# Two upright score tiles of a fused attention and feed-forward kernel made ordinary, and the order around them written anew

## The chip, the cores and the metric

The kernel runs on one core of a Trainium2 chip. A core has five engines with queues of their own: PE (matrix products), DVE and POOL (elementwise work and reductions), ACT (exponentials, casts) and SP, which here issues all DMAs. Each engine takes its instructions strictly in the order of its queue. The metric is the device time of one execution in microseconds; beside it stands one profiled execution.

## The reference, cut to what matters

```python
mask = q_assign[:, :, :, None] == k_assign[:, :, None, :]
scores = scale * np.matmul(q, k.transpose(0, 1, 3, 2))
scores = np.where(mask, scores, -1000000000.0)
scores = scores - np.max(scores, axis=-1, keepdims=True)
attn = np.exp(scores)
attn = attn / (np.sum(attn, axis=-1, keepdims=True) + 1e-09)
return np.matmul(attn, v).astype(np.float32)
...
h = x @ w_in
g = np.maximum(h, 0.0) + np.log1p(np.exp(-np.abs(h)))
return (g @ w_out).astype(np.float32)
```

q, k and v are 4 x 8 x 768 x 64 in float32, the two weight matrices come in float64; `q_assign` and `k_assign` are the nearest of 16 centroids per head. The attention's output, 3072 x 512, goes through a layer of 2048 hidden columns with softplus.

## The kernel before, in words

The work is cut into eight passes: a batch and one half of its 768 queries (three blocks of 128). A pass has 24 score tiles, one per head and query block, numbered through the program; tiles 24 to 47 are the second pass. Floats are split into a high and a low float16 part, so that a product is made of two or three float16 products. Besides the scores a pass makes, from the attention of its 24 tiles, 16 blocks of hidden rows (`ffn1`, f = 0 to 15, two halves each), their softplus, and the output (`ffn2`). The weights are converted and split step by step (`prep_weights`, steps 0 to 31) beside the first two passes. While tiles 34 to 47 are made, the hidden rows of the first pass and the weight steps 24 to 31 are worked on.

A score tile is made in one of two ways.
- Ordinary (`scores`): four products of 128x384 (L1051, scores of t), the row maximum on DVE (L1067), the exponential on ACT (L1075), its high part by a cast (L276, key `ph{t}`), the low part by a subtraction (L1089, key `p{t}`) on POOL or DVE, then one transposing DMA for a pair of tiles (L1101), and the attend: 18 float16 products (L1141 to L1143).
- Upright (`upright`): two products of 128x384 for the maxima (L942), the maximum on DVE (L954), a transposition of it on PE (L961), a shift row written by ACT or DVE (L967, L969, key `u{t}`), twelve products of 128x128 that give the scores already transposed (L981, L982), the exponential on ACT (L1025), and the attend in float32 (L1137). It needs no cast, no subtraction and no DMA.

Pairs of tiles listed in `UPRIGHT` are upright (`is_up`): pair 17 is tiles 34 and 35, head 3 with query blocks 4 and 5. An ordinary tile among upright neighbours needs a row of its query tile filled with zeros (`fill`, L798).

Scores are written to a ring of two PSUM buffers (tag `s`), hidden rows and cluster products to another ring of two (tag `h`), outputs to one buffer (tag `o`): a new product waits until the buffer's last reader is done. The hidden rows of f are read by an exponential and a logarithm on ACT (L1233, L1234) and a combination on DVE (L1249, here: the softplus of f), whose end frees the buffer.

The order of all operations is written out: `Order.run` walks the string `PLAN`, two characters per operation, each naming the coroutine whose next operation is issued. Nothing is reordered later. `either` chooses the engine of an operation: the first of two named, or the second where its key stands in `SWAPPED`.

Of the kernel before, what the change touches and what calls it, by code (L numbers as in the profile page):

```python
# [38 lines left out]
REBASE = 2.0**-112
SIGN_UP = 2.0**32  # L40
# [8 lines left out]
    "2927270d2b22220a222925cdce25242b2b29272d29260d0dcccbcccecd2d2729292fcf222b28cc0ace2f2h2f0d2d2f2d2bcb22cccgch"
    "ci2h2j2a0d0d0dcgcg2b2h2dcf0dcf0d0dcd2j2c2d2f2e0dcf0dcf0d0d22cjcd2fcbcb2h2e2e2e2l2j2j0d0d2l2n2nchci2echcgch2g"  # L50
    "2h2h2j2l2n2lcgcgck2jch2nce2p2p2i2l2k2p2l2r2ncicicjci2p2rcdchcl2ncjcj2m2p2t2r0eckckckck2t2p2rcj2e2ecicmcjce2o"
    "2r2r2v2v2t2q2t2v2t2q2q2qcl2x0e0e0e2v2tck2q2q2s2v2v2x2z2z2x2xcmclcmclcm2ucn2q2z312x312w0e0e0e0e0e0e0eco2z2x2z"
    "cl2z330e333131cl2y310fcncn0ecncz33353531cmcmcpcq33czcncococo33dpcn35cz37370f0f0fcoczdqdqdp35303937320e0e0eco"
    "cr0e333537dpcz0hdqdqdq3232323439czcp32cqcpcpcqcq32323539370f0f3b3936dsdsdsczcpcp3739crcq3b0fcrcrcrcr393d0fcz"
    "3bcz3b0ecs3d3d3b0f0f0f3dczdtdt0h3bdudu0f0fdtdt0hcqdt383d0i3d3f3f3aczctcscsducs3f3h3f3f3c3jcz3edv3h3jcscs0gcu"
    "0i0i0i3h3ld03hdwctct3h3hdw3edwcz3j0g3n3e3e3edwczd0ctcu3l3ndv0i3j3l3pdydyct3e3edwd0cu0g0j0kcucu3l3n3ndyczczdz"
    "3gdz0i3p0i0icz3rczcuctcv3l3j3l3p3t3p0g3ndzczdz0i3r3iczdzd03p3pcve0e03t3r3v0ie0cz3ke10jcvcv3tcz3xcve13te23md0"
# [1634 lines left out]
```

## Time and profile before

| what | us |
|---|---|
| median of three runs | 813.47 (812.93 to 814.27) |
| the profiled execution | 813.45 |
| its span, first to last instruction | 811.7 |
| PE busy / DVE / ACT / POOL | 799.6 / 599.2 / 548.7 / 471.5 |

The span is what the trace shows; 1.75 us of the execution lie around it. Busy is time in which an engine has any instruction recorded. Records of PE overlap, so that its work is read from the distances between starts.

### The profile page before, as it was taken

Reading aid. Unit: us, or ns where it says so; the run is one execution under the profiler, and the core shown is the slowest. Engines: PE = TensorE matmul, PEld = TensorE weight load, DVE = VectorE, ACT = ScalarE, POOL = GpSimd, SP = SyncE. Lnnn points to the kernel's source line nnn. Section 1 sums busy time; section 2 is a strip of 40 time slices with the busy share of each in tenths; the row PEclk is TensorE's granted clock in tenths of the full one; section 3 lists DMA queues with packets and bytes.
Section 4 is the critical chain, followed back from the end, with each engine's and each line's share of the span. In section 5 each row is a group of like instructions: output and inputs, shape, how many; then the busy total and the mean of one; then the engine's idle time right before and its main releaser. Section 6 shows DMA issues by size and latency. Waiting matters only on the chain.

```text
span 811.7 us, 19601 instructions
## 1 busy us (share of the span) xinstructions
PE 799.6 (99%) x8086; PEld 542.6 (67%) x8086; DVE 599.2 (74%) x1005; ACT 548.7 (68%) x851; POOL 471.5 (58%) x351
## 2 busy tenths in 40 slices
PE   8999999999999999999999999999999999999998
PEld 7898976655666666666666656666666656576787
DVE  6889998987976877756675547658555878887795
ACT  6677688865777777648587577677676667645441
POOL 4645455554756577745677685687578552613454
PEclk9999999999999999999999999999999999999999
DMA  9986769999899999999899999999888677830101
GB/s 259 234 184 165 205 151 216 195 227 204 165 190 182 180 202 196 215 204 177 153 177 177 185 185 175 209 203 179 171 159 176 116 143 131 131 60 1 47 1 59
DMA packets 390474, 133.71 MB, mean 165 GB/s; under 512 B 367088, under 2 KB 383984, under 8 KB 390384
## 3 DMA queue, kind: packets, MB, share of 16 engines
q1 hardware_dynamic: 390384, 132.46, 82.6%
q8 instruction: 63, 1.03, 0.5%
q14 instruction: 27, 0.22, 0.1%
HBM read 35.68 MB, written 6.29 MB: 52 GB/s over the span
## 4 chain that ended last, share of the span: by engine, by line
PE 76%; DMA 4%; DVE 3%; ACT 2%; issue 1%; POOL 0%; SPq 0%; DVEq 0%; POOLq 0%; ACTq 0%
PE s L1051 11%; PE h L1212 9%; PE h L1214 9%; PE h L1213 9%; PE o L1613 7%; PE o L1615 7%; PE o L1614 7%; DMA pt<-phl 4%; PE mbank L1141 3%; PE mbank L1143 3%; PE mbank L1142 3%; PE m L1490 2%; PE m L1492 2%; PE m L1491 2%; ACT phl L276 1%
## 5 line engine op out<-in xcount | busy, mean ns | idle before, releaser
L1089 POOL TENSOR_TENSOR phl<-p,phl 128x768 f16<-128x768 f32 x117 | 194.1, 1667 | 124.1 <-ACT phl L276 94.1
L1067 DVE TENSOR_REDUCE negm<-s 128x1 f32<-128x768 f32 x156 | 148.1, 953 | 50.3 <-PE s L1051 48.8
L1075 ACT ACTIVATE p<-s,negm 128x768 f32<-128x768 f32 x156 | 139.4, 896 | 64.4 <-DVE negm L1067 49.1
L1212 PE MATMUL h<-xT,wi 128*128 128x384 f16 x512 | 166.9, 326 | 1.1 <-DVE fg L1249 1.1
L1214 PE MATMUL h<-xT,wi 128*128 128x384 f16 x512 | 167.1, 326 | 0.0
L1213 PE MATMUL h<-xT,wi 128*128 128x384 f16 x512 | 167.0, 326 | 0.0
L276 ACT CAST phl<-p 128x768 f16<-128x768 f32 x145 | 118.7, 828 | 20.3 <-DMA pt<-phl 18.0
L1051 PE MATMUL s<-kt,qt 128*128 128x384 f16 x624 | 126.2, 326 | 0.3 <-ACT p L1075 0.3
L1233 ACT ACTIVATE fa<-h 128x384 f32<-128x384 f32 x128 | 62.2, 487 | 70.9 <-PE h L1214 70.2
L1613 PE MATMUL o<-wo,gh 128*128 128x512 f16 x288 | 109.2, 379 | 0.4 <-DVE ot L1636 0.4
L1615 PE MATMUL o<-wo,gh 128*128 128x512 f16 x288 | 109.2, 379 | 0.0
L1614 PE MATMUL o<-wo,gh 128*128 128x512 f16 x288 | 109.2, 379 | 0.0
L1249 DVE SCALAR_TENSOR_TENSOR fg<-fa,h 128x384 f32<-128x384 f32 x104 | 56.7, 549 | 61.6 <-ACT fa L1234 54.2
L1141 PE MATMUL mbank<-vb,pt 128*128 128x65 f16 x936 | 100.2, 193 | 0.6 <-DMA pt<-phl 0.4
L1142 PE MATMUL mbank<-vb,pt 128*128 128x64 f16 x936 | 100.3, 192 | 0.0
L1143 PE MATMUL mbank<-vb,pt 128*128 128x65 f16 x936 | 100.0, 194 | 0.0
L1141 PEld LDWEIGHTS <-pt 128*128 128x128 f16 x936 | 86.8, 98 | 12.9 <-DMA pt<-phl 2.3
L1142 PEld LDWEIGHTS <-pt 128*128 128x128 f16 x936 | 86.3, 97 | 10.4
L1272 POOL TENSOR_TENSOR gh<-fg,gh 128x768 f16<-128x768 f32 x43 | 71.9, 1673 | 28.1 <-ACT gh L276 28.0
L1143 PEld LDWEIGHTS <-pt 128*128 128x128 f16 x936 | 86.4, 97 | 0.0
L1051 PEld LDWEIGHTS <-qt 128*128 128x128 f16 x624 | 58.4, 98 | 40.3 <-issue 0.6
L1214 PEld LDWEIGHTS <-wi 128*128 128x128 f16 x512 | 50.0, 98 | 33.2
(300 smaller groups left out, 1621.2 us busy)
## 6 DMA issues: line engine op xcount, KB each, us to landing
...
pt<-phl SPq DMA_TRANSPOSE x78, 6.0
```

What stands on the lines that cost most here:

```text
L1051: nc.tensor.matmul(st[:, j, :SH], qt[:, s, i], kt[:, s, NT // 2 * j : NT // 2 * (j + 1)], start=(s == 0), stop=(s == 1),)
L1067: yield op("DVE", 950, lambda: nc.vector.tensor_reduce(negm, st[:, :, :SH], AX.XY, ALU.max, negate=True))
L1089: lambda e: e.tensor_tensor(phl[:, u, 1], p32, phl[:, u, 0], ALU.subtract),
L1141: nc.tensor.matmul(av, pt[:, 0, c], vb[:, c, D : 2 * D + 1], start=(c == 0), stop=False)
L1142: nc.tensor.matmul(av[:, :D], pt[:, 0, c], vb[:, c, :D], start=False, stop=False)
L1143: nc.tensor.matmul(av, pt[:, 1, c], vb[:, c, D : 2 * D + 1], start=False, stop=(c == NT - 1))
L1212: nc.tensor.matmul(hp, w[0], x[0], start=(c == 0), stop=False)
L1213: nc.tensor.matmul(hp, w[0], x[1], start=False, stop=False)
L1214: nc.tensor.matmul(hp, w[1], x[0], start=False, stop=(c == NP - 1))
L1613: nc.tensor.matmul(po, g[0], wo[:, f, 0, 0], start=(f == f0), stop=False)
L1614: nc.tensor.matmul(po, g[0], wo[:, f, 0, 1], start=False, stop=False)
L1615: nc.tensor.matmul(po, g[1], wo[:, f, 0, 0], start=False, stop=(f == f0 + NF // 2 - 1))
```

## The change

Pair 17 leaves `UPRIGHT`, so tiles 34 and 35 become ordinary. The keys `u34` and `u35` are gone with it, `ph34`, `ph35`, `p34` and `p35` come (POOL makes both subtractions, ACT both casts), one transposing DMA and one zero fill come. In `SWAPPED`, `p40` goes (its subtraction moves from DVE to POOL) and `w24`, `w25` (weight subtractions, POOL to DVE), `wh27` (a weight cast, ACT to POOL) and `xh1_1` (a cast of 128x384, ACT to POOL) come. `PLAN` differs from about the 370th of 3464 operations to the 1418th, which before ran from some 66 us to some 295 us. No function is changed.

```diff
-UPRIGHT = (0, 1, 2, 3, 4, 5, 6, 7, 8, 9, 10, 11, 12, 13, 14, 15, 16, 17)
+UPRIGHT = tuple(range(17))
...
-    "d0cz0mebebeb0m0ld0d0ebebea0gec3w0g0g0gcycy0gcycy0g0g0gd03yd040ea0gcy0g0g0g0ld0420od0424242424242eded0n0n0n0n"
+    "czebebebd0d0d0ebebea0gec3w3y0g0g0gcycy0gcycy0g0g0gd0d0d0eacy0g0g0g0g0m0m0l0ld0ed40424242424242420o0n0n0n0n0n"
```

The attends of tiles 34 and 35 go further back on PE. Before, from the scores of tile 37 to those of tile 39 (`s_4`, `s_5` and `s_3` are tiles 37, 38 and 39; `ptf_4` holds tiles 34 and 35; one row of each group of products is shown):

```order
L1051 MATMUL s_4_2145<-kt_593,qt_1_1557 128x384
...
L1137 MATMUL mbank<-rawv_131,ptf_4_2064 128x65 x6
...
L1051 MATMUL s_5_2151<-kt_593,qt_1_1557 128x384
...
L1212 MATMUL h_5_2088<-xT_985,wi 128x384
...
L1137 MATMUL mbank<-rawv_131,ptf_4_2064 128x65 x6
...
L701 MATMUL cnt_2142<-eq_k_2020,ones 128x192
...
L1051 MATMUL s_3_2197<-kt_593,qt_1_1557 128x384
```

Now:

```order
L1051 MATMUL s_4_2103<-kt_593,qt_1_1558 128x384
...
L1051 MATMUL s_5_2131<-kt_593,qt_1_1558 128x384
...
L1212 MATMUL h_5_2078<-xT_985,wi 128x384
...
L701 MATMUL cnt_2122<-eq_k_2005,ones 128x192
...
L1051 MATMUL s_3_2164<-kt_593,qt_1_1558 128x384
```

Both rows of L1137 have left this stretch; they come back as float16 attends behind the second half of f = 6.

POOL around the same place, before (`phl` are low parts of scores, `wo` weights, `gh` hidden rows, `kn` keys, `xn` the attention's output):

```order
L404 TENSOR_TENSOR wo<-wo 128x512
L1272 TENSOR_TENSOR gh_1_2089<-fg_1_1990,gh_1_2089 128x768
L1089 TENSOR_TENSOR phl_3_2146<-p_4_3_2125,phl_3_2146 128x768
L404 TENSOR_TENSOR wo<-wo 128x512
L631 TENSOR_TENSOR kn_10_2116<-rawk_2113,kn_10_2116 128x12x64
L1089 TENSOR_TENSOR phl_3_2146<-p_4_4_2183,phl_3_2146 128x768
L1178 TENSOR_TENSOR xn_1_2239<-x_3_1_2237,xn_1_2239 128x2x3x64
L1272 TENSOR_TENSOR gh_2_2220<-fg_2_2084,gh_2_2220 128x768
L404 TENSOR_TENSOR wo<-wo 128x512 x2
```

Now:

```order
L276 CAST wo<-wo 128x512
L1089 TENSOR_TENSOR phl_4_2008<-p_3_4_2003,phl_4_2008 128x768
L1089 TENSOR_TENSOR phl_4_2008<-p_3_5_2042,phl_4_2008 128x768
L1089 TENSOR_TENSOR phl_3_2126<-p_4_3_2106,phl_3_2126 128x768
L631 TENSOR_TENSOR kn_10_2093<-rawk_2014,kn_10_2093 128x12x64
L1089 TENSOR_TENSOR phl_3_2126<-p_4_4_2151,phl_3_2126 128x768
L1272 TENSOR_TENSOR gh_1_2079<-fg_1_1994,gh_1_2079 128x768
L1272 TENSOR_TENSOR gh_2_2187<-fg_2_2097,gh_2_2187 128x768
L276 CAST wo<-wo 128x512
L404 TENSOR_TENSOR wo<-wo 128x512
L276 CAST xn_1_2320<-x_3_1_2311 128x2x3x64
L404 TENSOR_TENSOR wo<-wo 128x512
```

Three subtractions of scores stand in a row where a weight, a hidden row, a score and a weight stood; a cast of weights and one of `xn` are new.

DVE from the maximum of tile 35 to that of tile 36, before (`eq_k` and `best_k` are the cluster operations of keys, `fg` the softplus, `vb` the values):

```order
L954 TENSOR_REDUCE negu_5_2028<-m_5_2018 128x1
L590 TENSOR_TENSOR eq_k_2020<-eq_k_2020,tab 128x192
L592 TENSOR_REDUCE best_k_2066<-eq_k_2020 128x12
L594 TENSOR_TENSOR eq_k_2020<-eq_k_2020,best_k_2066 128x192
L969 TENSOR_SCALAR qt_1_1106<-turned 1x128
L650 TENSOR_SCALAR kn_8_1783<-eq_k_2020 128x12x16
L1249 SCALAR_TENSOR_TENSOR fg_1_1990<-fa_3_2036,h_3_1992 128x384
L467 TENSOR_TENSOR vb_104<-rawv_1879,vb_104 128x12x64
L404 TENSOR_TENSOR wo<-wo 128x512
L1067 TENSOR_REDUCE negm_3_2123<-s_3_2047 128x1
```

Now:

```order
L1067 TENSOR_REDUCE negm_5_2015<-s_5_2000 128x1
L404 TENSOR_TENSOR wo<-wo 128x512
L590 TENSOR_TENSOR eq_k_2005<-eq_k_2005,tab 128x192
L592 TENSOR_REDUCE best_k_2045<-eq_k_2005 128x12
L404 TENSOR_TENSOR wo<-wo 128x512
L594 TENSOR_TENSOR eq_k_2005<-eq_k_2005,best_k_2045 128x192
L650 TENSOR_SCALAR kn_8_1784<-eq_k_2005 128x12x16
L1249 SCALAR_TENSOR_TENSOR fg_1_1994<-fa_3_2032,h_3_1996 128x384
L467 TENSOR_TENSOR vb_104<-rawv_1880,vb_104 128x12x64
L1067 TENSOR_REDUCE negm_3_2104<-s_3_2076 128x1
```

The weight subtraction (L404) of step 24 now stands ahead of the cluster operations, that of step 23 between them instead of behind `vb`, and a shift row is gone.

ACT early in the second pass, before (`turned` is the transposed maximum; L967 writes shift rows; the three in a row are those of tiles 16, 18 and 17):

```order
L967 ACTIVATE qt_0_609<-turned 1x128 x3
L390 ACTIVATE wi<-wo 128x512
L1025 ACTIVATE ptf_1_1310<-u_1_1265 128x768
L1025 ACTIVATE ptf_1_1310<-u_2_1336 128x768
L832 ACTIVATE n_112<-eq_q_1_1331 128x12x16
L276 CAST wi<-wo 128x512 x2
L1025 ACTIVATE ptf_0_1379<-u_0_1366 128x768
L276 CAST wi<-wo 128x512
L967 ACTIVATE qt_0_609<-turned 1x128 x2
```

Now:

```order
L967 ACTIVATE qt_0_609<-turned 1x128 x2
L390 ACTIVATE wi<-wo 128x512
L1025 ACTIVATE ptf_1_1309<-u_1_1265 128x768
L1025 ACTIVATE ptf_1_1309<-u_2_1334 128x768
L832 ACTIVATE n_112<-eq_q_1_1329 128x12x16
L276 CAST wi<-wo 128x512 x2
L967 ACTIVATE qt_0_609<-turned 1x128
L276 CAST wi<-wo 128x512
L1025 ACTIVATE ptf_0_1403<-u_0_1390 128x768
L276 CAST wi<-wo 128x512
L967 ACTIVATE qt_0_609<-turned 1x128 x2
```

The shift row of tile 18 has moved behind the exponential of tile 17, the cluster row `n` and two weight casts. On PE the attend of tile 17 stands ahead of tile 18's products in turn.

## Rows read from the trace of the kernel before

**Rows 1.** the page, busy time and share of the span, x instructions
```profile
PE 799.6 (99%) x8086; PEld 542.6 (67%) x8086; DVE 599.2 (74%) x1005; ACT 548.7 (68%) x851; POOL 471.5 (58%) x351
```

**Rows 2.** PE in order of time, 153 to 156: start, length, line, operands
```profile
153.46 0.81 PE L1051 MATMUL s<-kt,qt 128*128 128x384 f16 x4
154.10 0.19 PE L1141 MATMUL mbank<-vb,pt 128*128 128x65 f16 x1
...
154.65 0.38 PE L1613 MATMUL o<-wo,gh 128*128 128x512 f16 x1
```

**Rows 3.** PE's waits, whole program: total us, times, longest
```profile
PE h L1212 <- DVE fg L1249: 1.1, 3, 0.6
...
PE turned L961 <- ACT qt L967: 0.7, 2, 0.4
PE turned L961 <- DVE rs L1158: 0.5, 1, 0.5
...
PE o L1613 <- DVE ot L1636: 0.4, 1, 0.4
...
PE s L1051 <- ACT p L1075: 0.3, 1, 0.3
```

**Rows 4.** busy us of PE, PEld, DVE, ACT, POOL; clock, DMA
```profile
112.00:158.00 46.00, 44.81 (x399) 30.75 (x398) 41.56 (x62) 38.21 (x62) 23.26 (x19) 1.00 0.91 204
```

**Rows 5.** the chain that ends at 157, from 112, by line
```profile
by line: DMA rawk<-in_k_dram 10.6%; DVE wo L392 10.2%; issue 9.7%; ACT phl L276 7.3%; DVE negm L1067 7.0%; DVE wo L396 6.0%; DVE phl L1089 5.6%; DVE fg L1249 5.6%; ACT p L1075 5.4%; DVE eq_k L590 3.3%; PE h L1212 2.5%; PE h L1213 2.2%; PE h
```

**Rows 6.** PE in order of time, 90 to 94
```profile
90.81 1.45 PE L1137 MATMUL mbank<-rawv,ptf 128*128 128x65 f32 x12
92.09 0.22 PE L981 MATMUL u<-qt,kt 128*128 128x128 f16 x1
...
92.77 0.49 PE L942 MATMUL m<-kt,qt 128*128 128x384 f16 x2
...
93.20 1.45 PE L1137 MATMUL mbank<-rawv,ptf 128*128 128x65 f32 x12
```

**Rows 7.** ACT in order of time, 125 to 130; [idle before <- ended by]
```profile
125.64 0.90 ACT L1075 ACTIVATE p<-s,negm 128x768 f32<-128x768 f32 x1 [0.28 <-DVE negm L1067]
...
128.45 0.83 ACT L276 CAST kn<-rawk 128x768 f16<-128x768 f32 x1 [0.49 <-DMA rawk<-in_k_dram]
129.19 0.89 ACT L1075 ACTIVATE p<-s,negm 128x768 f32<-128x768 f32 x1
```

**Rows 8.** groups by line: count, busy us, mean ns, idle before
```profile
L1089 POOL TENSOR_TENSOR phl<-p,phl 128x768 f16<-128x768 f32 x117 | 194.1, 1667 | 124.1 <-ACT phl L276 94.1 <-issue 14.1 <-PE sim_k L563 5.2
...
L1025 ACT ACTIVATE ptf<-u 128x768 f32<-128x768 f32 x36 | 29.2, 810 | 17.2 <-PE u L982 17.0
```

**Rows 9.** DVE in order of time, 119 to 134
```profile
119.31 1.01 DVE L590 TENSOR_TENSOR eq_k<-eq_k,tab 128x192 f16<-128x192 f16 x1
...
123.06 0.69 DVE L404 TENSOR_TENSOR wo<-wo 128x512 f16<-128x512 f32 x1
...
125.53 0.42 DVE L392 TENSOR_SCALAR wo<-wo 128x512 int32<-128x512 int32 x1
...
131.93 1.80 DVE L392 TENSOR_SCALAR wo<-wo 128x512 int32<-128x512 int32 x1 [1.47 <-ACT wo L390]
```

**Rows 10.** POOL in order of time, 119 to 134
```profile
119.05 1.16 POOL L404 TENSOR_TENSOR wo<-wo 128x512 f16<-128x512 f32 x1
...
131.81 1.64 POOL L1089 TENSOR_TENSOR phl<-p,phl 128x768 f16<-128x768 f32 x1
```

**Rows 11.** DMA issues by line: count, us from issue to landing
```profile
pt<-phl SPq DMA_TRANSPOSE x78, 6.0
```

**Rows 12.** PE in order of time, 126 to 132
```profile
126.71 0.81 PE L1051 MATMUL s<-kt,qt 128*128 128x384 f16 x4
...
128.64 0.81 PE L1051 MATMUL s<-kt,qt 128*128 128x384 f16 x4
...
131.64 0.81 PE L1051 MATMUL s<-kt,qt 128*128 128x384 f16 x4
```

More of the change, by code (lines that the diff above doesn't have):

```diff
@@ new lines @@
+SWAPPED = ('E1_0', 'S1l_1', 'S1l_3', 'S2_1', 'S2_3', 'S2h_0', 'S2l_0', 'S3l_0', 'S3l_2', 'S4_0', 'S4_2', 'S4_3', 'S4h_2', 'S4l_1', 'S4l_2', 'T1a_0', 'T1a_2', 'T1c_0', 'T1c_3', 'T1h_3', 'T1l_1', 'T2a_2', 'T2c_1', 'T3a_0', 'T3a_1', 'T3a_2', 'T3a_3', 'T3b_0', 'T3b_1', 'T3b_2', 'T3c_1', 'T3l_1', 'T3l_3', 'T4c_0', 'T4h_2', 'T4h_3', 'T4l_0', 'T4l_2', 'g0_3', 'g0_5', 'g1_1', 'g2_5', 'g5_7', 'g6_0', 'g6_1', 'g6_4', 'g6_5', 'g6_6', 'g7_1', 'g7_2', 'g7_4', 'g7_5', 'g7_6', 'g7_7', 'gh1_6', 'gh2_4', 'gh3_1', 'gh5_6', 'gh7_0', 'gh7_2', 'gh7_3', 'gh7_5', 'k0_0', 'k0_1', 'k14', 'k18', 'k22', 'kT0_0_0', 'kT0_2_1', 'kT1_2_0', 'kT1_2_1', 'm12_2_0', 'm12_3_0', 'm20_4_0', 'm28_7_0', 'm8_2_0', 'm8_3_0', 'p100', 'p101', 'p103', 'p136', 'p170', 'p172', 'p173', 'p175', 'p177', 'p178', 'p180', 'p181', 'p182', 'p183', 'p184', 'p185', 'p186', 'p189', 'p190', 'p191', 'p38', 'p39', 'p42', 'p45', 'p46', 'p47', 'p59', 'p61', 'p64', 'p67', 'p71', 'p72', 'p79', 'p82', 'p85', 'p89', 'p90', 'p92', 'ph175', 'ph178', 'ph180', 'ph184', 'ph186', 'ph189', 'ph58', 'ph62', 'ph83', 'ph86', 'ph87', 'q0_0_0', 'qT1_1', 'u1', 'u11', 'u13', 'u21', 'u23', 'u27', 'u31', 'u33', 'u35', 'v8', 'vh14', 'vh18', 'w15', 'w19', 'w20', 'w23', 'w24', 'w25', 'w29', 'wh17', 'wh24', 'wh27', 'wh29', 'wh30', 'wh7', 'wh9', 'x0_2', 'x2_0', 'x6_3', 'x7_0', 'x7_1', 'x7_2', 'x7_3', 'xh0_3', 'xh1_1', 'xh1_3', 'xh2_3', 'xh3_0', 'xh3_3', 'xh6_3', 'xh7_0', 'zk10', 'zk12', 'zk16', 'zk18', 'zk2', 'zk20', 'zk4', 'zq0_1', 'zq8_2')
@@ L48 @@
     "1xc7c6c61zc61xc8c7c7c6c721211w23231z0a21211z1y210d252023ce0bcfc9cac8cbcc21caca25252723c822c9c9c8ca2723c92325"
[L49 to L57, printed above, removed]
@@ L58 @@
-    "0j3vcvcw3t3re13x3r3t3v3z3zcze1e1e3e3e3e30k0k0k3x3ocze4cw3q3qcz413q3qcwcw0i3ze4e4e4cxcze53qd00n3x0i0i3ve5cwcz"
-    "cwe4d0cze7e73x3s3v3x3qe5e6d0410mcye7czczcxcxcxcxcxe60g3u0ke7e7e8d0e9e941410ke9cz0k0k0k0k0k413z3z410k0n0n3q0n"
-    "d0cz0mebebeb0m0ld0d0ebebea0gec3w0g0g0gcycy0gcycy0g0g0gd03yd040ea0gcy0g0g0g0ld0420od0424242424242eded0n0n0n0n"
-    "0n0n0n0n0l0l0n0kd0d04343434343eed045cz4545454545eeczef4747474747cz494949494949efd0egczeheh4b4b4b0o0oefd04d4d"
-    "4dehehd00l0l0l0l4f4f0l0ld04b4b4d4d4f444h4h4h4hd0eiei4j4j4j464dcz0l0l0l0l4h4l4l4f4fehczejejej48cz4a4hcz0l4n4n"
@@ L63 @@
-    "czcz4l4p0p0l4cekekek4p4ecz4e4l4l4j4j4lel4nekekelel4e4e4p4p4pczd0cz4g0p0pem4eemem4e4eem4n4nemczenen4r4r4r4ieg"
-    "4p4t4t4tczd0enen4v4v4r4r4k4x4x4t4t4v4v4v4x4mczeoeo4t4z4zczeoeo51514zczepep4o0p534q4qep4x4x4xcz51d04q4q4q4q53"
-    "535555eo4z4z4sczeq51510p574u514q57eqeq55czd0ereqeq0p0p0p0p57cz53534w59594yeseses5555550p0p5b5b0p0p0p0p0p0pd0"
+    "2927270d2b22220a222925cdce25242b2b29272d29260d0dcccbcccecd2d2729292fcf222b28cc0ace2f2h2f0d2d2d2bcb22cccgch2h"
+    "2j2a0d0d0dcgcg2b2h2dcf0dcf0d0dcd2j2c2d2e2e2ecg2e0dcf0dcicf0d0d0d22cjce2f2fcd2fcbcb2h2l2j2j0d0d2l2n2nchcichch"
@@ new lines @@
+    "2h2g2h2j2l2n2lcgcgck2jch2n2p2p2e2e2i2l2k2p2l2r2ncicicjci2p2rchcl2ncjcj2m2p2t2r0eckckckckcd2t2p2rcj2ecicmcjce"
+    "2o2r2r2v2v2t2q2t2v2t2q2q2qcl2x0e0e0e2t2vck2q2q2s2v2v2x2z2z2x2xcmclcmclcm2ucn2q2z312x312w0e0e0e0e0e0e0eco2z2x"
+    "2zcl2z330e333131cl2y310fcncn0ecncz33353531cmcmcpcq33czcncococo33dpcn35cz37370f0f0fcoczdqdqdp35303937320ecocr"
+    "33350e0e0e0e37dpcz0hdqdqdq3939323232czcp32cqcpcpcqcq32323534370f390f3b36dsdsdscpcp37cr3b0f3bcq3d0fcrcrcrczcz"
+    "cz3b3dcr0f0fcz39cq0fdtdt0h3ddu0f39dt3b3d0h3d380icsdu0f3f3f3aczctcsducscs3f3h3f3d3f3jczdv3hcscs3j0gcu0i0i0i3h"
@@ new lines @@
+    "3ld0ctdx3hct3h3hdxdtdxcz3jdx0g3nczdydyctcudt3c3ed03l3n0gdvdycz0i3l3j3pctdxd03ecu0j3e0kcucucu3l3e3n3ncvczdz3r"
+    "0i0idz0i3e3p3jcz3g3iczct3l3l3p3t3p0g0idzczdz3r3nczdzd03p3pe0e03t3r3vcve0czcz3ke10i0jcvcv3t3t3xcve1e23md00j3e"
+    "3vcvcw3t3re13x3r3t3v3z3zcze1e1e3e3e3e30k3z0k0k3xcz3ocwe43q3qcz413q0i3qcwcwe4e4e4e4cxcze5e5e53qd0d00n3x0i0i3v"
+    "cwczcwcze7e73x3s3v3x3qe6d0410mcye7czczcxcxcxcxcxe60g3u0ke7e7e8d0e9e941410ke9cz0k0k0k0k0k413z3z410k0n0n0n3e3q"
+    "czebebebd0d0d0ebebea0gec3w3y0g0g0gcycy0gcycy0g0g0gd0d0d0eacy0g0g0g0g0m0m0l0ld0ed40424242424242420o0n0n0n0n0n"
@@ new lines @@
+    "0n0n0n0n0kd0d0d0ee43430l0l43434345d0cz4545454545eeczeg474747474749czed4949eg494949efczeheh4b4b4b0o0oegd04d4d"
+    "4dehehd00l0l0l0l4f4f0l0ld04b4b4d4d4f444h4h4h4hd04j4j4j464dcz0l0l0l0l4h4l4l4f4fehczejeieiejej48cz4a4hcz0l4n4n"
+    "4l4p0p0l4cekczczekek4p4ecz4e4l4l4e4e4j4j4l4nelekekelel4p4p4pczd0cz4g0p0pem4eemem4e4eem4n4nemczenen4r4r4r4i4p"
+    "ef4t4t4tczd0enen4v4v4r4r4k4x4x4t4t4v4v4v4x4mczeoeo4t4z4zczeoeo51514x4zczepepep4o0p534q4q4x4xcz51d04q4q4q4q53"
+    "535555eo4z4z4sczeq51510p574u514q57eqeq55czd0ereqeq0p0p0p0p57cz53534w59594yeses5555es550p0p5b0p5b0p0p0p0p0pd0"
@@ L68 @@
     "0q0q0q0q0qd05t5g5n5r5td05i5p5p5pexex0q0qex5r5v5vez5t5t5t0q5v5r5r5k5x5xcz5m5tczf0f0f00r0r5xex5z5z5z5v5vczd0cz"
-    "f1f1f15x5x5o61cz6161635q5q5q5q5q5q610r63czf2f2f2d05x65655scz5z5z0r610r0r0r0r0t0u6367czd05u6165f3f1f169f3670r"
+    "f1f1f15x5x5ocz5q5q61635q61615q5q5q610r63czf2f2f2d05x65655scz5z5z0r610r0r0r0r0t0u6367czd05u6165f3f1f169f3670r"
     "f30r695wcz63635yczd0f36565650t0t670u0u0s0uf4f4f469cz6b6b6bczf6f66d0w6df667676d5qcz60czf7f76b6d62626262f569f3"
```

1 line of the change is left out of this document (removed).

## The prediction

> **What bounds the kernel now.** I read the engines' shares first: PE has a record running for 799.6 of 811.7 us, at the full granted clock (the 2.4 GHz level), the next engine DVE for 599.2 [rows 1]. That share cannot be read as work, because records overlap: the records of four score products span 0.81 us, yet the next group begins 0.64 us after they did [rows 2]. So I read starts, not durations, and then PE's waits: those that fall in or near this change's stretch (66 to 295 us) are 1.1 for DVE's softplus, 0.7 for ACT's shift rows, 0.5 for DVE's row sums and 0.4 for DVE's accumulator, all small [rows 3]. By that, PE is the bound and whatever leaves PE leaves the time. The stretch in which tiles 34 to 46 are made says something else. From 112 to 158 us DVE is busy 41.6 of 46 and ACT 38.2 [rows 4], and the chain that ends there runs through DVE, ACT and one load; PE's lines have a few per cent each [rows 5]. There PE, DVE and ACT move in step, and PE runs ahead by little.
>
> **The change part by part.** *PE.* An upright tile costs PE, from start to start, 1.28 for the float32 attend (90.81 to 92.09), 0.68 for twelve score products (to 92.77), 0.43 for two maximum products and the transposition (to 93.20): 2.39 [rows 6]. An ordinary one costs 0.64 for four products (153.46 to 154.10) and 0.55 for eighteen (to 154.65): 1.19 [rows 2]. Two tiles: -2.40 of PE work.
>
> *ACT, DVE, POOL, DMA.* ACT gets two casts of 0.83 and two exponentials of 0.90 [rows 7] in place of 0.81 [rows 8], together +1.83, and gives up a shift row, a weight cast and a 128x384 cast, each shorter than a cast of 0.83: between 0 and +1.8, near +0.4. DVE gives up a subtraction of 128x768 and a shift row and takes two of 128x512 at 0.69 [rows 9]: about even. POOL gets three subtractions of 1.67 [rows 8] and two casts, and gives up two of 1.16 [rows 10]: +2.7 without the casts, +4.3 if each cost 0.83 as on ACT. One transposing DMA more (6.0 from issue to landing [rows 11]) is covered: the attends of 34 and 35 now stand behind the scores of 38 to 40 and the hidden rows f = 5 and 6. The zero fill of 3 KB is issued tens of us before tile 34 needs it. I cost both at nothing; without that cover the flip would cost what it is late, up to its 6.0.
>
> *Middle, what goes.* After the attend of tile 31, PE waited for the softplus of f = 2, about 0.4 (1.1 in three such waits [rows 3]). The scores of tile 35 now stand between, so it goes: -0.4.
>
> *Middle, what comes.* A score tile has two PSUM buffers, so the scores of t start only when the exponential of t-2 is done. Before, the attends of 34 and 35 (1.28 each) stood between the scores of 37 (126.71) and of 39 (131.64), 4.93 apart [rows 12]. Without them PE is there after 4.93 - 2.56 = 2.37. The exponential of 37 ended at 130.08, 3.37 after its scores began [rows 7, 12]. So scores 39 wait 1.0. This is no accident of one load: kn's cast waited 0.49 for DMA there [rows 7], whose load is now issued earlier, but from the end of exponential 36 (126.54) to that of 37 is still 3.54 - 0.49 = 3.05 of ACT's own row (cast, weight cast, cast, exponential), and 36 comes no earlier than DVE lets it. I take +1.2.
>
> DVE first: up to about 119.4 its queue holds the same kinds of instruction in another order, behind the same holds by POOL, and stands where it did. Behind it now stand two weight subtractions, the cluster operations, softplus and v's subtraction, and then the maximum of 36. Before, all of that but one weight subtraction, and a shift row more, ran without a break from 119.31 to 123.75, and 0.7 of it was a hold-up that I come to [rows 9]. Taken alone it would now end near 123.4 (123.75 - 0.7 - 0.3 + 0.61), and the maximum of 36 near 124.3. PE reaches the scores of 38 at 128.64 - 1.28 (attend 34) - 0.94 (two tiles' products: 2 x (1.11 - 0.64)) - 0.4 (the wait that went) = 126.0 [rows 2, 6, 12], after the exponential: no wait. But DVE and POOL hold each other up: a DVE operation of 0.42 took 1.80 when it began at 131.93 beside a POOL subtraction that ran from 131.81 to 133.45, and ended 0.28 after it; one of the cluster operations took 1.01, ending 0.11 after POOL's (119.05 to 120.21) [rows 9, 10]. The new subtraction of tile 34 starts on POOL right behind the weight's cast, at about 119.2, a tenth before DVE's weight subtraction, which waits for the same cast: DVE loses 1.5. The one of tile 35 starts near 123.4, half a us before v's on DVE: 1.2 more. The maximum of 36 then ends near 126.8, its exponential 0.9 later, and scores 38 wait 1.75 (126.8 + 0.9 + 0.05 - 126.0). Bounds of these two meetings: 0 (DVE is first in both) and 2 x 1.64; I take 1.75 on PE, by the row at 131.93. Near 147 the moved subtraction of tile 40 and the two moved casts do the same to the softplus of f = 7, which f = 9 waits for: 0 to 1.64, taken 1.0. The wait of some 0.7 for softplus f = 5 stays, since it follows exponential 37 on ACT. The waits at 148 to 156 (0.3 for an exponential [rows 3], 0.8 with those beside it) go, since there ACT sets the time and PE comes later.
>
> The Trainium skill (SBUF — State Buffer, its part on the two sides of SBUF) calls DVE's and POOL's shared port pair an exclusive lock, held for the whole instruction by whichever starts first. The rows at 131.93 and 119.31 agree [rows 9, 10]. It speaks against this change, which gives POOL more work beside DVE: by that rule the two engines' meetings cost DVE what is left of POOL's instruction, and the sum is the one below; if they only shared the port's speed, it would lie nearer to the first rival.
>
> *Before and behind it.* On ACT the shift row of tile 18 moves behind an exponential, a cluster row and two casts, and the attend of 17 goes ahead of 18's products; PE's wait for ACT's shift rows (0.7 in two [rows 3]) grows by about an exponential (0.81 [rows 8]), and the wait of 0.5 for DVE's row sums some 13 us later [rows 3] takes that much back: +0.3; bounds 0 and 1.28, the attend that changed places. Near 187 two attends and a cluster product now stand between the fourth accumulation and the next one, which waited for DVE's accumulator (0.4 [rows 3], 0.6 with what it dragged): -0.6.
>
> **Sum**: -2.40 - 0.4 + 1.2 + 1.75 + 1.0 - 0.8 + 0.3 - 0.6 = +0.05. Against the profiled execution's 813.45 (span 811.7 and 1.75 around it) that is 813.5; the median of the three runs shown is 813.47, the same to 0.01%.
>
> **The rivals.** *PE keeps its gain.* PE's share speaks for it, and DVE's idle time at 124 to 132. If DVE wins the port in all three meetings, the waits of 1.75 and 1.0 are gone: 813.5 - 2.75 = 810.8; with the 2.40 alone, 811.05. Against it: POOL's subtraction needs no semaphore from another engine behind the cast, DVE's does.
>
> *DVE falls further behind: slower.* The place is tiles 38 to 41. POOL now runs the subtraction of 36, that of kn and that of 37 with no room between, and DVE's moved weight subtraction and its shift for the next weight both fall beside them. If the second is also held for a whole 1.64, the softplus of f = 5 and with it f = 6 come 1.64 later; and if the early shift row costs the full 1.28, 1.0 more than the sum has: 813.5 + 1.64 + 0.98 = 816.1. It decides from the point where the maximum of 36 ends later than about 126.8 against the old time. For it: POOL gains about 4 us in a stretch where DVE is busy 90%. Against it: POOL was idle half of that stretch (busy 23.3 of 46 [rows 4]).
>
> *Nothing on the bound moves*, because DVE and ACT pace the middle: that is the forecast's own case, and without the small terms before and behind it 813.8.
>
> **How the numbers follow.** A measurement of this kernel can tell about 0.2% (1.6 us) from no change. I give the forecast's case 0.54 (its own range 812.2 to 814.9), PE keeps its gain 0.23, slower 0.23. The time is that of the first, 813.5. Its neighbours lie at 810.8 and 816.1; the range 811.0 to 816.0 leaves out the outer parts of both. Under 811.8 lies the first rival: faster 0.23; over 815.1 the second: slower 0.23; same 0.54.
>
> **What would show it.** PE's busy share of matmul work falls by 2.4 in any case. Right: a PE wait of over 1 us ended by ACT's exponential (line 1075) ahead of the scores of 38 or 39, DVE's weight subtraction (line 404) near 119 lasting over 1.5, and the wait for the accumulator near 187 gone. Wrong: PE without such waits between 120 and 150 (then 811); or softplus waits (line 1249) that add up to over 3 us there (then 816). If tile 34's attend waits for its flip, the cover that I gave the DMA was wrong.

## The result and the profile after

| kernel | median us | range | profiled execution |
|---|---|---|---|
| before | 813.62 | 812.93 to 814.27 | 813.45, span 811.7 |
| changed | 820.35 | 817.97 to 821.79 | 820.58, span 818.8 |

The ratio is 1.0079 (95% interval 1.0063 to 1.0094): slower by 6.7 us, where 813.5 (811.0 to 816.0) was forecast. One execution below, of 886 us, ran at a granted clock of 0.88 and is left out as slow.

The page after, busy time and share of the span, x instructions:

```profile
PE 798.8 (98%) x8076; PEld 540.8 (66%) x8076; DVE 608.9 (74%) x1005; ACT 549.3 (67%) x850; POOL 478.1 (58%) x354
```

PE's busy time is only 0.8 under [rows 1]; records overlap, so its work is read from starts below. DVE's busy time grew by 9.7 with the same count of instructions. Summed over its operations, each against the length that it has undisturbed, 9.3 of that is operations that lasted longer.

PE's waits after (total us, times, longest), where [rows 3] had 0.3 for the exponential and 1.1 for the softplus:

```profile
PE s L1051 <- ACT p L1075: 3.4, 3, 2.2
PE h L1212 <- DVE fg L1249: 2.8, 2, 1.5
PE turned L961 <- ACT qt L967: 1.7, 2, 1.5
PE mbank L1141 <- DVE x L1166: 1.5, 1, 1.5
```

Lost time of PE, as used from here on, is read from starts. I took PE's operations in order, each with the distance from start to start that it has where nothing waits (0.64 for a score tile, 0.97 for half a hidden row, 1.28 for a float32 attend), and summed what went beyond it. The stretches (us) are in each kernel's own time; the second profiles are experiments below.

| PE's lost time, us | 0-60 | 60-112 | 112-160 | 160-236 | 236-264 | 264-410 | 410-440 | 440-end |
|---|---|---|---|---|---|---|---|---|
| before | 7.2 | 3.0 | 1.9 | 0.6 | 0.7 | 0.0 | 0.4 | 0.4 |
| before, second profile | 8.1 | 3.1 | 0.5 | 0.6 | 0.9 | 0.0 | 0.8 | 0.6 |
| changed | 8.4 | 4.2 | 4.9 | 0.6 | 1.7 | 0.0 | 4.1 | 0.1 |
| changed, second profile | 7.8 | 4.2 | 4.7 | 0.7 | 1.8 | 0.0 | 4.1 | 0.0 |

The first column varies by 1 us from one profile to the next, with the landing of the first keys. Before loses most of what it gains there again at 112 to 160 (7.2 + 1.9 and 8.1 + 0.5), so the second profile of before is the better one to compare with. Against it the changed kernel loses 1.1 at 60 to 112, 4.4 at 112 to 160 (2.4 of which is the work that PE was spared), 0.8 near 259 and 3.3 near 424. Against the first profile the lost time grew by 9.8 in all and the span by 7.1: PE's work fell by 2.7, where 2.40 was worked out, and the loss is in waits.

**112 to 160.** DVE's weight subtraction of step 24, 0.69 long in [rows 9], met the subtraction of tile 34 on POOL and was held to 2.08, as priced; the second meeting went the other way: v's subtraction on DVE was first, and POOL's subtraction of 35 took 2.38 in place of 1.67 [rows 8]. DVE, then POOL, in order of time:

```profile
121.21 2.08 DVE L404 TENSOR_TENSOR wo<-wo 128x512 f16<-128x512 f32 x1
...
125.34 0.95 DVE L467 TENSOR_TENSOR vb<-rawv,vb 128x768 f16<-128x768 f32 x1
126.20 0.95 DVE L1067 TENSOR_REDUCE negm<-s 128x1 f32<-128x768 f32 x1
```
```profile
121.10 1.65 POOL L1089 TENSOR_TENSOR phl<-p,phl 128x768 f16<-128x768 f32 x1
125.41 2.38 POOL L1089 TENSOR_TENSOR phl<-p,phl 128x768 f16<-128x768 f32 x1 [2.67 <-ACT phl L276]
```

The exponential of 36 ended at 128.15 and PE's scores of 38 began at 128.29: no wait there. The scores of 39 and both later hidden rows waited (PE, idle time and what ended it):

```profile
131.16 0.81 PE L1051 MATMUL s<-kt,qt 128*128 128x384 f16 x4 [1.00 <-ACT p L1075]
134.56 0.32 PE L1212 MATMUL h<-xT,wi 128*128 128x384 f16 x1 [1.30 <-DVE fg L1249]
...
150.34 0.32 PE L1212 MATMUL h<-xT,wi 128*128 128x384 f16 x1 [1.55 <-DVE fg L1249]
```

**415 to 430, where no operation changed its place.** Before, ACT's casts of tiles 112 and 113 waited 0.90 for a transposing DMA to free their buffer; POOL's subtraction therefore began when DVE's short cluster operations were nearly done (ACT, DVE, POOL):

```profile
416.19 1.56 ACT L276 CAST phl<-p 128x768 f16<-128x768 f32 x2 [0.90 <-DMA pt<-phl]
```
```profile
416.20 0.36 DVE L594 TENSOR_TENSOR eq_q<-eq_q,best_q 128x192 f16<-128x192 f16 x1
416.59 0.24 DVE L834 TENSOR_SCALAR n<-eq_q 128x192 f16<-128x192 f16 x1
416.87 0.36 DVE L914 TENSOR_TENSOR eq_q<-eq_q,al 128x192 f16<-128x192 f16 x1
```
```profile
417.15 3.25 POOL L1089 TENSOR_TENSOR phl<-p,phl 128x768 f16<-128x768 f32 x2 [1.48 <-ACT phl L276]
```

After, the casts wait for nothing, POOL is there first, and three operations of 0.2 to 0.4 take 5.05 together; the maximum of 114 behind them comes late, then its exponential, then PE's scores of 116 (DVE, POOL, PE):

```profile
419.96 1.80 DVE L594 TENSOR_TENSOR eq_q<-eq_q,best_q 128x192 f16<-128x192 f16 x1
421.79 1.56 DVE L834 TENSOR_SCALAR n<-eq_q 128x192 f16<-128x192 f16 x1
423.38 1.69 DVE L914 TENSOR_TENSOR eq_q<-eq_q,al 128x192 f16<-128x192 f16 x1
...
425.38 0.95 DVE L1067 TENSOR_REDUCE negm<-s 128x1 f32<-128x768 f32 x1
```
```profile
419.89 3.36 POOL L1089 TENSOR_TENSOR phl<-p,phl 128x768 f16<-128x768 f32 x2 [0.47 <-POOL xn L1178]
```
```profile
427.37 1.27 PE L1051 MATMUL s<-kt,qt 128*128 128x384 f16 x4 [2.24 <-ACT p L1075]
```

Behind that wait the granted clock fell to its 1.2 GHz level for some 3 us (the column after POOL's is the clock), which cost 1.7 more:

```profile
424.00:428.00 4.00, 1.76 (x9) 0.74 (x7) 3.85 (x6) 1.57 (x3) 2.33 (x2) 0.95 1.02 192
428.00:432.00 4.00, 4.00 (x32) 2.21 (x30) 1.75 (x3) 3.74 (x5) 2.36 (x2) 0.63 0.68 127
```

Near 255, where two pairs of neighbours on DVE had changed places, the same happens to two such operations, and the attend of 66 waits 1.51 for DVE to write out the head before it:

```profile
255.22 1.52 DVE L834 TENSOR_SCALAR n<-eq_q 128x192 f16<-128x192 f16 x1
256.77 1.69 DVE L914 TENSOR_TENSOR eq_q<-eq_q,al 128x192 f16<-128x192 f16 x1
```

**Why the DMA lands earlier.** The DMA that frees the buffer lands 7.19 after its issue at 408.92 before, and 5.47 after its issue at 412.69 after. In the DMA view of 408.9 to 416.2 before, and of 412.6 to 418.2 after (GB/s in 40 slices, then the queues that moved something):

```profile
GB/s 215 164 39 45 275 66 34 182 215 205 102 10 250 290 288 286 265 234 227 217 219 215 219 209 215 219 177 24 98 0 0 0 0 0 0 0 0 0 8 178
...
q8 instruction: 1, 0.02, 0.8%
```
```profile
GB/s 168 62 13 11 68 289 89 0 2 95 207 216 221 214 210 208 218 212 221 216 216 214 218 218 212 227 223 219 218 216 216 218 219 212 201 125 7 0 0 0
...
q1 hardware_dynamic: 3518, 0.88, 94.4%
```

Before, the 98 GB/s slice is followed by nothing for some 1.6 us. One packet of queue q8, a load of 16 KB of instructions, begins 5.18 after the issue and takes 0.93 of that time; after, there is no such packet in the window. The page counts 63 of them for 16,152 products and weight loads of PE, one for about 256. (The Trainium skill, Perfetto Trace Analysis, The 4-stage abstract model, gives 64 bytes for an instruction; by an estimate from that figure 256 fill 16 KB, and the trace's count agrees.) I counted over the transposing DMAs of score pairs whose landing is recorded, taking in the 8 KB loads of a second instruction queue, q14. In before, 22 of the 46 in whose flight a load began took over 6.8 us, and none of the 32 others; after, 20 of 40 and none of 32. A load in flight is thus not enough by itself: half of these DMAs were not late. The change takes 20 instructions out of PE's program, so every later load falls at a later operation: 5.99 after the issue near 412, 6.62 near 248 (before 5.27).

### The profile page after: what moved, and what is told of

The parts are those of the page before. It is cut to its first block, busy times and chain, and to the rows that moved or that the text cites. A ratio compares the mean times of both kernels' runs of the same rounds, so it can differ in the third digit from the quotient of the medians.

```text
span 818.8 us, 19592 instructions
## 1 busy us (share of the span) xinstructions
PE 798.8 (98%) x8076; PEld 540.8 (66%) x8076; DVE 608.9 (74%) x1005; ACT 549.3 (67%) x850; POOL 478.1 (58%) x354
## 4 chain that ended last, share of the span: by engine, by line
PE 77%; DVE 5%; DMA 2%; ACT 1%; issue 0%; POOL 0%; SPq 0%; ACTq 0%
PE s L1051 11%; PE h L1212 9%; PE h L1213 9%; PE h L1214 9%; PE o L1613 7%; PE o L1615 7%; PE o L1614 7%; PE mbank L1143 3%; PE mbank L1141 3%; PE mbank L1142 3%; PE m L1492 2%; PE m L1491 2%; PE m L1490 2%; DMA wo<-in_moe_w_out_dram 1%; DMA rawq<-in_q_dram 1%; DVE negm L1067 1%
## 5 line engine op out<-in xcount | busy, mean ns | idle before, releaser
L1089 POOL TENSOR_TENSOR phl<-p,phl 128x768 f16<-128x768 f32 x120 | 200.4, 1677 | 123.6 <-ACT phl L276 89.8
L1067 DVE TENSOR_REDUCE negm<-s 128x1 f32<-128x768 f32 x158 | 149.9, 952 | 45.1 <-PE s L1051 44.6
L276 ACT CAST phl<-p 128x768 f16<-128x768 f32 x147 | 120.4, 828 | 20.2 <-DMA pt<-phl 18.1
L1051 PE MATMUL s<-kt,qt 128*128 128x384 f16 x632 | 127.9, 327 | 3.4 <-ACT p L1075 3.4
L1142 PEld LDWEIGHTS <-pt 128*128 128x128 f16 x948 | 87.3, 97 | 12.1 <-issue 1.7
L1141 PEld LDWEIGHTS <-pt 128*128 128x128 f16 x948 | 87.9, 98 | 10.8
L1143 PEld LDWEIGHTS <-pt 128*128 128x128 f16 x948 | 87.5, 97 | 0.0
```

Source lines behind the costliest of these rows:

```text
L1051: nc.tensor.matmul(st[:, j, :SH], qt[:, s, i], kt[:, s, NT // 2 * j : NT // 2 * (j + 1)], start=(s == 0), stop=(s == 1),)
L1067: yield op("DVE", 950, lambda: nc.vector.tensor_reduce(negm, st[:, :, :SH], AX.XY, ALU.max, negate=True))
L1089: lambda e: e.tensor_tensor(phl[:, u, 1], p32, phl[:, u, 0], ALU.subtract),
L1141: nc.tensor.matmul(av, pt[:, 0, c], vb[:, c, D : 2 * D + 1], start=(c == 0), stop=False)
L1142: nc.tensor.matmul(av[:, :D], pt[:, 0, c], vb[:, c, :D], start=False, stop=False)
L1143: nc.tensor.matmul(av, pt[:, 1, c], vb[:, c, D : 2 * D + 1], start=False, stop=(c == NT - 1))
```

## The experiments

Each ratio is against the kernel before on the same chip: 812.67 for the first four experiments, 813.03 for the next four, then 813.15, and 813.11 for the last.

**The changed kernel again.** Nothing edited.

> The changed kernel once more, nothing altered. Its first profile is 7.1 us longer than that of before: about 1.1 at the start (a first load of keys that lands 0.9 later), 1.2 near 73 (PE waits for ACT's shift row of tile 18), 0.5 net over 112 to 158, 1.3 near 259 and 3.7 near 424. Theory A: the waits near 259 and 424 belong to the kernel: there the transposing DMAs issued near 248 and 412 land after 5.5 us (7.2 in the kernel before), because no load of PE's instructions falls among their packets; the subtraction on POOL then starts earlier and meets a row of short cluster operations on DVE. By A both waits stand again, and the time is 820 again (819 to 821.5). Theory B: the landings are chance: one or both waits are gone in this profile, and single times spread over 815 to 821. The start's 1.1 is expected to be chance in both: it should not be there in every profile.

818.36 (817.64 to 820.21), ratio 1.0070 (1.0058 to 1.0082). The landings are 5.55 and 5.48 again and both waits stand (table above): theory A, though the time is under its 819. Single times still spread over 2.6 us. The mean granted clock of each execution shows why. Of the changed kernel's twelve, six in the result and six here, seven stand at 0.998 and took 819.2 to 821.8; five stand at 0.999 or 1.000 and took 817.6 to 818.8. Five of the result's six are of the first kind, and two of the six here, so the stretch at 1.2 GHz accounts for most of the difference between 6.7 and 5.7. The start's part was 0.6 less.

**Ten more idle products on PE.**

```diff
-FILL = {0: 40, 3: 12, 4: 21, ...
+FILL = {0: 40, 3: 22, 4: 21, ...
```

> The changed kernel with ten more idle products on PE in its first microseconds (the second entry of the table of filling products 22 in place of 12), in a stretch where PE waits 1.2 us for its first similarity product, so that they cost nothing there. PE's program is then one instruction short of the length that it has in the kernel before from tile 34 on, and loads of PE's instructions (63 of 16 KB for some 16,150 instructions, one for every 256) fall at the same operations as in the kernel before. Theory A (instruction loads decide how early two transposing DMAs land, and so whether POOL meets DVE's cluster operations): the two landings are near 7.2 again, the waits of 1.3 near 259 and 3.7 near 424 shrink to below 0.5 each: 820.4 - 1.3 - 3.3 = 815.8 (815 to 817). Theory B (the new order itself puts POOL and DVE together there): both waits stay, 820.4 (819.5 to 821.5).

815.73 (815.40 to 816.32), ratio 1.0036 (1.0024 to 1.0048): 2.6 faster by *adding* instructions. Loads begin 5.35 and 5.20 after the two issues, the landings are 7.35 and 7.21, lost time is 0.8 at 236 to 264 and 0.6 at 410 to 440: theory A. ACT waits for the landing again, and DVE's operations are short (ACT, then DVE):

```profile
417.85 1.56 ACT L276 CAST phl<-p 128x768 f16<-128x768 f32 x2 [0.94 <-DMA pt<-phl]
```
```profile
417.82 0.36 DVE L594 TENSOR_TENSOR eq_q<-eq_q,best_q 128x192 f16<-128x192 f16 x1
418.22 0.24 DVE L834 TENSOR_SCALAR n<-eq_q 128x192 f16<-128x192 f16 x1
418.50 0.36 DVE L914 TENSOR_TENSOR eq_q<-eq_q,al 128x192 f16<-128x192 f16 x1
```

**The kernel before with ten fewer.**

```diff
-FILL = {0: 40, 3: 12, 4: 21, ...
+FILL = {0: 40, 3: 2, 4: 21, ...
```

> The kernel before with ten idle products fewer on PE in its first microseconds (2 in place of 12), where PE waits anyway. Nothing else is altered, no operation changes its place; PE's instructions are loaded at later operations, by about 20 of 256, as in the changed kernel. Theory A: in one or both of the stretches near 252 and 416 a transposing DMA lands after 5.5 in place of 7.2, POOL's subtraction meets the cluster operations on DVE, and the kernel before gets slower without any change of its order: 813.6 + 1 to 4 = 814.6 to 817.6. Theory B: the same as before, 813.6 within 0.7.

819.55, ratio 1.0072 (1.0056 to 1.0088); single times 816.1 to 820.3. Theory A, more than it asked for: the kernel before is as slow as the changed one, with its order untouched. Landings 5.58 and 5.55, lost time 1.9 and 2.4 in the two stretches. DVE, then PE:

```profile
417.32 1.80 DVE L594 TENSOR_TENSOR eq_q<-eq_q,best_q 128x192 f16<-128x192 f16 x1
419.15 1.56 DVE L834 TENSOR_SCALAR n<-eq_q 128x192 f16<-128x192 f16 x1
420.75 1.69 DVE L914 TENSOR_TENSOR eq_q<-eq_q,al 128x192 f16<-128x192 f16 x1
```
```profile
424.73 0.81 PE L1051 MATMUL s<-kt,qt 128*128 128x384 f16 x4 [2.24 <-ACT p L1075]
```

The profiled execution (816.14, mean clock 1.000) was its fastest; the other four, 1.7 to 4.2 longer, all stand at 0.998. A stretch at 1.2 GHz as long as the one above would cost 1.7 of that; where the rest is lost was not seen.

**The old order early.** From 66 to about 90 us all engines have the order of before again. ACT, where the shift rows of 16, 17 and 18 stand together again:

```diff
-L967 ACTIVATE qt_0_609<-turned 1x128 x2
+L967 ACTIVATE qt_0_609<-turned 1x128 x3
...
-L967 ACTIVATE qt_0_609<-turned 1x128
```

> The changed kernel with the old order of PE, DVE, ACT and POOL from 66 to about 90 us (shift row of tile 18 ahead of that of 17, attend of 17 behind the products of 18, and the casts and weight subtractions around them); tiles 34 and 35 and all that follows stay as changed. My reading: the wait of 1.6 for ACT's shift rows near 74 falls to 0.4, and 1.2 comes off the time: 819.2 (818.4 to 819.8). Rival 1: what comes earlier there waits at 112 to 135 for DVE and ACT, which pace that stretch: 820.4. Rival 2: the shift by 1.2 alters which of POOL's and DVE's operations meet later, by 1 to 4 us in either sense; then the waits near 259 and 424 differ in the profile.

818.96 against 818.36: nothing gained. Lost time at 60 to 112 fell from 4.2 to 3.7 only; the wait before 77 was replaced by 0.8 before 80 and 0.7 before 92.

**DVE's order at the two meetings.** Two maxima and a softplus go ahead of the short operations. The maxima near 255 (near 420 alike):

```diff
 L592 TENSOR_REDUCE best_q_3_3989<-eq_q_3_3922 128x12
+L1067 TENSOR_REDUCE negm_1_3995<-s_1_3957 128x1
+L1067 TENSOR_REDUCE negm_2_4011<-s_2_4005 128x1
 L594 TENSOR_TENSOR eq_q_3_3922<-eq_q_3_3922,best_q_3_3989 128x192
```

> The changed kernel with DVE's order altered in two places only: near 255 the maximum of tile 71 and the softplus of f = 11, near 420 the maxima of tiles 114 and 115 and a softplus, come ahead of short cluster operations that nobody waits for soon. Instruction loads and landings stay as they are. If the waits of 1.7 near 259 and 2.4 near 424 (and the 1.2 GHz level for some 4 us behind the second) come from maxima that stand on DVE behind cluster operations held by POOL's subtractions, they go: 818.4 of this chip - 1.4 - 3.3 = 813.7 to 816, near 815.3. Rival: the late maxima are late for another reason (the subtraction or the landing itself paces ACT), then 818.4 within 0.8.

816.63, ratio 1.0040 (1.0028 to 1.0052), where the changed kernel stands at 1.0070 to 1.0079: between the two forecasts. Near 420 the lost time is gone (0.0 of 4.1) though the landing is still early (5.46): the row of held operations was the cause. Near 259, 1.1 of 1.7 stays; I had named a maximum there, but the attend of 66 waits for DVE's output of the head before, which still stands behind those operations. 0.5 and 0.7 appeared near 292 and 443.

**The same on the kernel before with fewer idle products.**

> The kernel before with ten idle products fewer at the start (819.6 against 812.7) and the same two alterations of DVE's order. If loads of instructions act on the time only through the two meetings of POOL and DVE, it is back at the time of before or under it: its profile had waits of 0.2 over 112 to 158 where before had 1.6, so 811.3 (810.5 to 813). Rival: fewer idle products cost time by themselves, at the start, or the cluster operations, now later, delay a transposition that the next pass's scores wait for: 814 to 819.

815.77, ratio 1.0037 (1.0023 to 1.0050), from 1.0072: half of it came back, not all, and the time lies in the rival's range. So the two meetings are not all that the loads of instructions act by. Lost time in the profile (814.12) is 0.8 near 258, 0.0 near 420, and 0.5 and 0.8 near 282 and 291. Single times run from 813.8 to 818.9; five of the twelve stand at a mean clock of 0.997 or 0.998 and took 815.8 to 818.8, and what they lose was not seen.

**Less work on POOL** (with ten more idle products).

```diff
-SWAPPED = ('E1_0', 'S1l_1', ... 'wh27', ... 'xh1_1', ...
+SWAPPED = ('E1_0', 'p40', 'S1l_1', ...
```

> The changed kernel with ten more idle products (815.7), and of its five changes of engine three taken back: the subtraction of tile 40 to DVE, the weight cast of step 27 and the cast of 128x384 to ACT. POOL's work between 140 and 147 falls by 1.16 to 2.8 us. Theory P (the port that DVE and POOL share sets the late softplus of f = 7: DVE's subtractions of 38 and 39 and a cluster operation last 1.9, 2.4 and 1.7 there): f = 9's wait of 1.45 falls under 0.5, 814.6 (814 to 815.3). Theory Q (DVE and ACT are full there): the work that they get back costs as much, 815.7 to 816.7.

814.00, ratio 1.0007 (0.9999 to 1.0016): 1.0 over before on this chip, where ten idle products alone stood 3.1 over before on theirs, so 2.1 less (1.7 by the bare medians): theory P. The wait before f = 9 is gone, since DVE's three subtractions take 3.16 where two took 4.21 in the changed kernel:

```profile
142.44 3.16 DVE L1089 TENSOR_TENSOR phl<-p,phl 128x768 f16<-128x768 f32 x3
145.52 0.25 DVE L590 TENSOR_TENSOR eq_k<-eq_k,tab 128x192 f16<-128x192 f16 x1
145.69 0.54 DVE L1249 SCALAR_TENSOR_TENSOR fg<-fa,h 128x384 f32<-128x384 f32 x1
```

The rows of the changed kernel that these answer to, with POOL's beside them:

```profile
144.00 4.21 DVE L1089 TENSOR_TENSOR phl<-p,phl 128x768 f16<-128x768 f32 x2
148.13 1.69 DVE L590 TENSOR_TENSOR eq_k<-eq_k,tab 128x192 f16<-128x192 f16 x1
```
```profile
145.04 2.36 POOL L1089 TENSOR_TENSOR phl<-p,phl 128x768 f16<-128x768 f32 x1
147.77 1.94 POOL L1089 TENSOR_TENSOR phl<-p,phl 128x768 f16<-128x768 f32 x1 [0.37 <-ACT phl L276]
```

**The pair alone.** Besides these two lines only the pair's own operations move in `PLAN`; `SWAPPED` stays as before.

```diff
-UPRIGHT = (0, 1, 2, 3, 4, 5, 6, 7, 8, 9, 10, 11, 12, 13, 14, 15, 16, 17)
+UPRIGHT = tuple(range(17))
-FILL = {0: 40, 3: 12, 4: 21, ...
+FILL = {0: 40, 3: 22, 4: 21, ...
```

> The kernel before with pair 17 made ordinary and the least else: scores and maxima of 34 and 35 stand where their maximum products stood (35 behind the attend of 31), their exponentials where the shift row of 34 and the exponential of 35 stood, both subtractions on POOL ahead of that of 36, the attends behind f = 6, the other engines' order and all choices of engine as before; ten more idle products at the start, so that instruction loads fall as in before. PE's work is 2.4 less. Theory R (the new order and the engine changes cost): the pair alone keeps most of its gain, 810.8 (810.3 to 811.8). Theory S (ACT, DVE and POOL pace this stretch, whatever the order): the 2.4 turn into waits for exponentials and softplus, 812.7 to 815.

823.45, ratio 1.0126 (1.0111 to 1.0142): neither theory. Lost time at 112 to 160 is 9.3: the wait below, and behind it the 1.2 GHz level for some 7 us. The exponential of 36 stands on ACT behind a weight's conversion whose load came late (ACT, then PE):

```profile
130.76 0.66 ACT L390 ACTIVATE wo<-wo 128x512 f32<-128x512 f32 x1 [5.13 <-DMA wo<-in_moe_w_out_dram]
```
```profile
132.26 1.44 PE L1051 MATMUL s<-kt,qt 128*128 128x384 f16 x4 [5.10 <-ACT p L1075]
```

That load takes its buffer from the ring of two in which the parts of score pairs lie (`ring("phl", 2)`); pair 17 now takes one too. The changed kernel has no such wait and is faster, so its new order and engines around the pair are worth more than they cost; which part of them avoids the wait was not tried. Both late meetings came back here too (1.8 and 4.1), the loads falling 6.24 and 5.44 after the issues: equal numbers of instructions did not keep them in place once PE had lost 9.3 before. That part of the expectation failed; the landings went with the loads as elsewhere (5.51, 5.48).

**The kernel before again.** Nothing edited.

> The kernel before, nothing altered, for a second profile. The profiles of eight kernels since then lost 0.5 to 1.5 us more over the first 60 us than the one of before (7.2 there), in waits for the first loads of keys, though none altered more there than some idle products. If that is chance of an execution, this profile shows 7.5 to 8.5 over the first 60 us too, and the start has no part in the difference of the two kernels. The waits of 0.4 near 252 and 427 and the landings of 7.2 are expected again, the time 812.2 to 813.6.

812.90, ratio 0.9995 (0.9984 to 1.0006). The start lost 8.1, landings 7.32 and 7.24; its profile is in the table.

**ACT and DVE reordered from 124 to 140 us**, on the version with less work on POOL. ACT's first rows:

```diff
+L276 CAST kn_10_2103<-rawk_2024 128x12x64
 L390 ACTIVATE wo<-wo 128x512
...
-L276 CAST kn_10_2103<-rawk_2024 128x12x64
```

> The changed kernel with ten more idle products and three engine changes taken back (814.0 against 813.0 of before), and ACT and DVE reordered from 124 to 140 us: the cast of keys comes into an idle stretch of ACT before the exponential of 36, the exponential and logarithm of f = 5 directly behind the exponential of 37, that of 39 earlier, and on DVE the softplus of f = 5 and 6 ahead of weight work. Three waits stood there: 1.16 (scores 39 for the exponential of 37), 1.06 (f = 6 for softplus 5), 0.47 (f = 7 for softplus 6). Theory 1: they are matters of order; they fall to 0.8 in all, and the time to 812.1 (811.3 to 812.8), under before. Theory 2: ACT and DVE have no room there, the waits come back within the next 30 us: 813.4 to 814.5. Rival to both: what follows comes 2 us earlier, loads of instructions fall elsewhere and POOL meets DVE near 253 or 417: 815 or more.

813.75, ratio 0.9998 (0.9988 to 1.0008): theory 2. The three waits fell to 0.7, and one of 2.0 for the transposed keys took their place (PE):

```profile
139.78 0.42 PE L560 MATMUL sim_k<-cents,kt 128*128 128x32 f16 x10 [1.97 <-DMA kt<-kn]
```

**With the old order early.**

> The same, and the old order from 66 to 90 us (shift row of tile 18 ahead of that of 17). Alone it brought nothing that could be measured on the changed kernel (819.0 against 818.4). Its wait of 1.6 near 74 fell to 0.3, but 0.8 and 0.7 stood near 80 and 90. If that balance holds, 812.1 as without it (811.2 to 812.8); if the new order's wait is a net loss of 0.7, 811.4.

813.86, ratio 1.0002 (0.9992 to 1.0013): no difference, as without that base.

**With the keys' products later.** Of its two edits the second bears on that wait; the expectation named the counts' buffer, the trace the keys.

```diff
-L560 MATMUL sim_k_2278<-cents,kt_2102 128x32
 L1051 LDWEIGHTS qt_1_1568
```

> The reordered version once more, with one reduction of counts (the line 713 of the clusters of keys) on DVE ahead of the cast chain of queries instead of behind it, and the similarity product of the next keys on PE (and its three operations on DVE) behind the scores of 41. In the version before it one wait of 2.1 stood in the way: f = 7 waited for the second buffer of hidden rows, which the counts of clusters held until that reduction ended at 138.4, behind an operation on the queries that waits for a load. Theory 1 (order): that wait falls under 0.5, nothing as long replaces it up to 160, and the time is 813.75 - 1.8 = 812.0 (811.2 to 812.6), under before's 813.0. Theory 2 (no room on ACT and DVE there): 1.5 or more of waits stand elsewhere between 130 and 160, 813.4 to 814.3.

813.63, ratio 1.0007 (0.9998 to 1.0016). The wait for keys went, and 1.4 for an exponential stood at 142.7: theory 2 again. No version beat the kernel before.

## Why the prediction was wrong

- **The step that failed** is the end of the sum: "Near 187 two attends and a cluster product now stand between ... -0.6", and then the sum. All behind that was put at nothing, without a reason, though the order differs up to some 295 us. The runs show 4.1 there against before's second profile (0.8 near 259, 3.3 near 424), and by the idle products alone, which change no order, 2.6 of the time came off (815.73 for 818.36), and 6.9 came on to the kernel before (819.55 for 812.67). Near 424 the order is the old one. The sum lacked the term "instructions that leave PE's program move the loads of all later ones".
- **The mechanism of the slower rival was right, its place was not.** "DVE falls further behind" priced the port at tiles 38 to 41. The held operations that cost most stood in the third and the fifth pass (near 255 and 420), on rows of DVE that I had not looked at. The Trainium skill (SBUF — State Buffer, its part on the two sides of SBUF) calls the port an exclusive lock; DVE's 1.80 that began 0.07 behind POOL's subtraction, and ended 0.2 behind the end of the first of the two, agrees.
- **The signs were too few.** All three signs of being right came, or nearly: 1.00 for an exponential ahead of the scores of 39, the weight subtraction at 2.08, the accumulator's wait gone. They lie between 119 and 187 and say nothing of what follows. The softplus waits came to 2.85, just under the 3 that stood for 816.
- **PE's work, -2.40**: right (2.7, from 9.8 and 7.1 above).
- **Scores 39, +1.2**: 1.2 in lost time (1.00 as an idle row). **f = 9, +1.0**: 1.7, the port as forecast, mis-sized by 0.7, since DVE's subtractions of 38 and 39 were both held too.
- **Scores 38, +1.75**: 0. Of the two meetings DVE lost one and was first in the other, and PE came later than worked out, by the start and by the shift row, so that the exponential of 36 was done. What was saved there stood before f = 6 (1.5 where 0.7 was to stay) and f = 7 (0.5). Lost time in the stretch was 4.9, where before's 1.9 and the terms add up to 4.65: right in sum by luck, not by place. And the 1.9 was partly chance: it is 0.5 in before's second profile.
- **The shift row, +0.3** (bounds 0 and 1.28): 1.1 from 60 to 112, near the upper bound. Undoing it gained nothing: other waits took its place (0.8 and 0.7).
- **Near 187, -0.6**: that wait went, and 0.4 before the scores of 51 came; the stretch 160 to 236 loses 0.6 as before: 0.
- **That ACT and DVE pace the middle**: borne out as far as tried. Two reorderings moved the waits and left 2.4 to 3.0 of lost time at 112 to 160.

In sum: of the 5.7 of the repeated measurement, the loads of instructions explain 2.6 (818.36 to 815.73) and POOL's added work 2.1 (3.1 over before to 1.0). The last 1.0 (814.00, not told from 813.03) is not settled. Also open is why moving the loads cost the kernel before 6.9 and the changed one only 2.6, and what sets whether the clock falls, which makes most of the difference between 6.7 and 5.7.
